# Value products of a threshold attention taken once per visit, with the last 64 keys of two heads in four 64x64 tiles, and one rotation of four PSUM banks

## The chip, the cores and the metric

One core of one Trainium2 chip. The metric is device time in microseconds (us) of one execution on that core; lower is better. TensorE's granted clock, the share of full speed that the chip's throttle allowed, was 0.982 to 0.995 over a whole run.

## The reference, cut to what matters

```python
# q, k, v: (8 batches, 8 heads, 576, 64) float32; tau = 0.02
scores = scale * np.matmul(q, k.transpose(0, 1, 3, 2))
thresh = np.max(scores, axis=-1, keepdims=True) - tau
scores = np.where(scores >= thresh, scores, -1000000000.0)
scores = scores - np.max(scores, axis=-1, keepdims=True)
attn = np.exp(scores)
attn = attn / (np.sum(attn, axis=-1, keepdims=True) + 1e-09)
attn_out = np.matmul(attn, v)
# bridge: (B, H, S, D) -> (B*S, H*D) = (4608, 512)
h = x @ w_in            # 512 x 2048
r = np.maximum(h, 0.0)
out = (r * r) @ w_out   # 2048 x 512
```

576 queries or keys are four blocks of 128 and a rest of 64. That rest is what the change is about.

## The kernel before

The kernel walks through *visits*. A visit is a pair of heads of one batch, in five *steps*: four of 128 queries for each head, and one with the last 64 queries of both. A step computes scores on TensorE, maxima and thresholds on VectorE, exponents on ScalarE and the division on GpSimd. The weights must then be transposed so that keys lie on partitions. The first visits do it on TensorE. The last 25 visits do it in two moves: VectorE transposes 32x32 squares into a buffer `turned`, and SyncE issues transfers that put the squares into their places in `wT`.

```python
NC9 = 2 * NBLK + 1                                   # 4 + 4 whole chunks, one shared chunk of last keys
wT = const.tile([P, NC9, S], FP32, name="wT")
NB = 2 * KB * 2 * 32                                 # KB = 18 blocks of 32 keys
turned = const.tile([P, 2 * NB], FP32, name="turned")   # two slots
...
def turn_blocks(vis, i):                             # VectorE, one step after the scores
    if not two or i % 2 == 0:
        at = len(blocks) % 2 * NB                    # the slots are used in turn
    ...
    for u in range(2 if two else 1):
        nc.vector.transpose(wb[:, u * KB:(u + 1) * KB, i % 2, :], w[:, u, :].rearrange("p (k q) -> p k q", q=32))

def place_blocks(vis, pair):                         # 16 transfers of SyncE
    for qb in range(4):
        for j in range(4):
            ...
            nc.sync.dma_start(out=to[:, :, at:at + 64], in_=wb[rows, j::4, :, :].rearrange("p c u q -> p c (u q)"))
```

A visit fills three such buffers: *pair 0* (steps 0 and 1), *pair 1* (steps 2 and 3) and the *rest* (step 4). With two slots, pair 0 of the next visit comes to lie where pair 1 of this visit was. VectorE may therefore turn it only when pair 1's transfers have read it.

The value products, before, came in two groups per visit, for different columns of `wT`. The fifth key chunk was padded with zeros in `vs` to 128 rows:

```python
def mix(n, cols):
    ps = bank[4] if by_dma(n) else take("tx", (4, 5))
    for c in range(NBLK + 1):
        for u in range(2):
            cw = NBLK if c == NBLK else u * (NBLK + 1) + c
            nc.tensor.matmul(ps[u * D:(u + 1) * D, 0:nq], vs[n % 2][:, u * (NBLK + 1) + c, :], wT[:, cw, cols],
                             start=(c == 0), stop=(c == NBLK))
...
mixed = {1: (0, 4), NBLK: (2, 4)}      # columns 0-255 four steps after step 1; 256-575 four after step 4
...
turn_blocks(m, x)
if x % 2 or x == NBLK:
    place_blocks(m, x // 2)
```

Between these, TensorE works off *pieces* of the feed-forward layer (one piece is 8 passes, 1.73 us; a pass is one of the two instructions of which every fp32 matmul consists), at a rate that the program works out from how many are waiting.

Of the kernel before, what the change touches and what calls it, by code (L numbers as in the profile page):

```python
# [19 lines left out]
def kernel(  # L20
# [10 lines left out]
    nc = tc.nc  # L31
# [38 lines left out]

    NC9 = 2 * NBLK + 1
# [4 lines left out]
    for i in range(2):  # L76
        nc.gpsimd.memset(vs[i], 0.0)
# [18 lines left out]
    p1s = const.tile([P, HD], FP32, name="p1s")  # L96
    u_sum = const.tile([P, HD], FP32, name="u_sum")
# [68 lines left out]
    def load_v(n):  # L166
# [4 lines left out]
        for u in range(2):  # L171
            at = u * (NBLK + 1)
            queue.dma_start(out=t[:, at:at + NBLK, :],
                              in_=v[b, h + u, 0:NBLK * P, :].rearrange("(c p) d -> p c d", p=P))
            queue.dma_start(out=t[u * D:(u + 1) * D, at + NBLK, :], in_=v[b, h + u, NBLK * P:S, :])
# [68 lines left out]
    used = {"tx": 0, "mm": 0}  # L244

    def take(what, among):
        used[what] += 1
        return bank[among[used[what] % len(among)]]

# [24 lines left out]
    blocks = {}  # L274

    def turn_blocks(vis, i):
# [12 lines left out]
        for u in range(2 if two else 1):  # L289
            nc.vector.transpose(wb[:, u * KB:(u + 1) * KB, i % 2, :], w[:, u, :].rearrange("p (k q) -> p k q", q=32))  # L290

    def place_blocks(vis, pair):

        wb = blocks[vis, pair]
        for qb in range(4):
            rows = slice(qb * 32, qb * 32 + 32)
            for j in range(4):
                to = wT[j * 32:j * 32 + 32, :, :]
                if pair < NBLK // 2:
                    at = pair * 2 * P + qb * 64  # L300
                    nc.sync.dma_start(out=to[:, :, at:at + 64], in_=wb[rows, j::4, :, :].rearrange("p c u q -> p c (u q)"))  # L301
                else:
# [4 lines left out]
                    at = NBLK * P + qb % 2 * 32  # L307
# [3 lines left out]

    def mix(n, cols):

        b, pr = divmod(visits[n][0], HP)
        nq = cols.stop - cols.start
        ps = bank[4] if by_dma(n) else take("tx", (4, 5))
        for c in range(NBLK + 1):
            for u in range(2):
                cw = NBLK if c == NBLK else u * (NBLK + 1) + c
                nc.tensor.matmul(ps[u * D:(u + 1) * D, 0:nq], vs[n % 2][:, u * (NBLK + 1) + c, :], wT[:, cw, cols],  # L320
                                 start=(c == 0), stop=(c == NBLK))
        lo = b * S + cols.start
        assert lo + nq - RING <= read_to["x"]

        def to(first, count):
            at = (lo + first) % RING
            assert at + count <= RING
            return xT[:, pr, at:at + count]

        whole = (lo % RING) + nq <= RING  # L330
        if by_dma(n):
            src = ps[:, 0:2 * P].rearrange("p (b u q) -> p b u q", u=2, b=4)
            if whole:
                nc.scalar.copy(to(0, 2 * P).rearrange("p (u b q) -> p b u q", u=2, b=4), src)  # L334
            else:

                for u in range(2):
                    fit = min(max((RING - lo % RING - u * P) // 32, 0), 4)
                    for b0, b1 in ((0, fit), (fit, 4)):
                        if b0 < b1:  # L340
                            nc.scalar.copy(to(u * P + b0 * 32, (b1 - b0) * 32).rearrange("p (b q) -> p b q", q=32),
                                           src[:, b0:b1, u, :])
            if nq > 2 * P:
                nc.scalar.copy(to(2 * P, nq - 2 * P), ps[:, 2 * P:nq])
        else:
            fit = nq if whole else RING - lo % RING
            for x0, x1 in ((0, fit), (fit, nq)):
                if x0 < x1:
                    nc.scalar.copy(to(x0, x1 - x0), ps[:, x0:x1])
# [3 lines left out]
    ring3 = [6, 5, 7]  # L353
# [7 lines left out]
    def mlp_in(j, x):  # L361

        f, at = FORDER[x], j * TCH % RING
        pair = x // 2
        if x % 2 == 0:
            used["h"] = take("mm", (6, 7)) if j < PLAIN else bank[ring3[pair % 3]]
# [55 lines left out]
    def product(j, x, half):  # L422

        if x == 0 and half == 0:
# [275 lines left out]
```

## Time and profile before

| | before |
|---|---|
| median of three runs | 1431.0 us (1430.79 to 1433.61) |
| profiled execution | 1429.3 us |
| TensorE busy | 97% |
| VectorE / ScalarE / GpSimd busy | 60% / 30% / 50% |

### The profile page before, as it was taken

To read this page: it belongs to the slowest core of one execution; us is meant where nothing else is said; L and a number is where in the kernel's file an instruction comes from. 1 tells how busy PE (TensorE), PEld (TensorE's weight loads), DVE (VectorE), ACT (ScalarE), POOL (GpSimd) and SP (SyncE) were. 2 spreads that over 40 slices of the span, in tenths; PEclk is the share of its full clock that TensorE was granted. 3 is DMA by queue.
4 is the path that set the end of the run, shared out by engine and by line. 5 is a ranking of instruction groups with operands and counts; after the bars stand their busy time and mean duration, and the time that the engine had idled before them with its cause. 6 is when DMAs were issued, how large, how long until landed. Compare 5 with 4: busy or idle time off the path is not lost.

```text
span 1429.3 us, 22123 instructions
## 1 busy us (share of the span) xinstructions
PE 1380.3 (97%) x7460; PEld 1067.1 (75%) x7460; DVE 860.0 (60%) x1781; ACT 435.2 (30%) x1063; POOL 720.3 (50%) x933
## 2 busy tenths in 40 slices
PE   5898989999999999999999999999999999999998
PEld 3676656777777777777777777778777777788887
DVE  5998986875657565657566656566656665621011
ACT  3765655223222222232223222222222232210100
POOL 3687877645464545354545445555445354531321
PEclk9998989999999999999999999999999999999999
DMA  7663441445454554454555554544455445430000
GB/s 148 128 139 102 126 120 42 76 72 101 89 100 84 106 96 95 81 106 80 103 90 110 96 95 84 109 84 96 86 110 93 92 84 107 78 71 15 0 15 15
DMA packets 503839, 125.93 MB, mean 88 GB/s; under 512 B 494928, under 2 KB 495728, under 8 KB 503728
## 3 DMA queue, kind: packets, MB, share of 16 engines
q1 hardware_dynamic: 494448, 107.42, 41.0%
q0 software_dynamic: 6896, 16.82, 3.8%
q8 instruction: 60, 0.98, 0.3%
q10 hardware_dynamic: 2384, 0.30, 0.1%
q14 instruction: 51, 0.42, 0.1%
HBM read 48.63 MB, written 9.44 MB: 41 GB/s over the span
## 4 chain that ended last, share of the span: by engine, by line
PE 81%; DVE 6%; SPq 5%; issue 3%; ACT 2%; DMA 1%; POOL 1%; ACTq 0%; DVEq 0%; POOLq 0%
PE bank L369 33%; PE bank L438 24%; PE s L201 12%; PE bank L320 10%; SPq L301 3%; SPq L308 1%; PE bank L259 1%; PE bank L403 1%; DVE w L229 1%; DVE turned L138 1%; SPq L162 1%; DVE st L206 1%; ACT wT L260 1%; DVE turned L290 1%; DVE turned L137 1%
## 5 line engine op out<-in xcount | busy, mean ns | idle before, releaser
L369 PE MATMUL bank<-xT,w_in_sb 128*128 128x256 f32 x2304 | 521.2, 383 | 1.6 <-ACT osb L410 1.6
L369 PEld LDWEIGHTS bank<-xT,w_in_sb 128*128 128x128 f32 x2304 | 432.9, 190 | 82.2 <-issue 22.3
L206 DVE TENSOR_REDUCE st<-s 128x1 f32<-128x576 f32 x288 | 207.0, 753 | 308.7 <-PE s L201 308.7
L229 DVE SCALAR_TENSOR_TENSOR w<-s,st,w 128x576 f32<-128x576 f32 x269 | 207.5, 804 | 75.6 <-ACT w L217 75.3
L241 POOL TENSOR_SCALAR w<-w,st 128x576 f32<-128x576 f32 x269 | 238.5, 894 | 26.9 <-DVE st L232 18.9
L438 PE MATMUL bank<-wo,gsum 128*128 128x256 f32 x1088 | 249.3, 382 | 0.0
L438 PEld LDWEIGHTS bank<-wo,gsum 128*128 128x128 f32 x1088 | 204.4, 190 | 38.4 <-issue 9.6
L380 POOL TENSOR_TENSOR g<-g 128x512 f32<-128x512 f32 x144 | 150.5, 1046 | 155.9 <-ACT g L379 138.5
L201 PE MATMUL s<-kT,qT 64*128 64x288 f32 x1024 | 180.2, 446 | 38.8 <-DVE w L229 16.9
L438 PE MATMUL bank<-wo,g 128*128 128x256 f32 x816 | 188.3, 381 | 0.0
L239 POOL TENSOR_SCALAR st<-st 128x2 f32<-128x2 f32 (+1 forms) x160 | 39.0, 244 | 295.5 <-DVE w L229 284.2
L217 ACT ACTIVATE w<-s,st 128x576 f32<-128x576 f32 x269 | 184.9, 733 | 0.6 <-ACT st L215 0.4
L320 PE MATMUL bank<-wT,vs 128*64 128x128 f32 (+3 forms) x1700 | 178.1, 357 | 2.6 <-ACT wT L260 2.4
L201 PEld LDWEIGHTS s<-kT,qT 64*128 64x128 f32 x1024 | 102.0, 193 | 99.7 <-issue 70.7
L438 PEld LDWEIGHTS bank<-wo,g 128*128 128x128 f32 x816 | 153.5, 190 | 27.8 <-issue 5.3
L290 DVE STREAM_TRANSPOSE turned<-w 128x576 f32<-128x576 f32 x225 | 162.1, 753 | 5.2 <-POOL w L241 5.1
L320 PEld LDWEIGHTS bank<-wT,vs 128*64 128x64 f32 x1700 | 104.7, 140 | 75.9 <-issue 22.1
L379 ACT ACTIVATE g<-bank 128x512 f32<-128x512 f32 x144 | 86.1, 598 | 205.8 <-PE bank L369 205.7
L214 ACT ACTIVATE st<-st 128x2 f32<-128x2 f32 (+1 forms) x160 | 33.3, 208 | 324.8 <-DVE st L206 324.2
L334 ACT COPY xT<-bank 128x256 f32<-128x256 f32 x42 | 15.6, 372 | 284.1 <-PE bank L320 284.1
L451 DVE TENSOR_TENSOR gsum<-g 128x512 f32<-128x512 f32 x34 | 22.6, 693 | 107.7 <-PE bank L438 107.7
L184 POOL COPY qmid<-qT 64x64 f32<-64x64 f32 x64 | 18.2, 285 | 101.8 <-DVE qT L180 99.9
(69 smaller groups left out, 963.9 us busy)
## 6 DMA issues: line engine op xcount, KB each, us to landing
wT<-turned SPq DMA_DIRECT2D x800, 72.0 KB, 2.2
ql<-in_q_dram SPq DMA_DIRECT2D x126, 72.0 KB, 2.5
out_dram<-osb POOLq DMA_DIRECT2D x34, 256.0 KB, 2.8
wo<-in_moe_w_in_dram SPq DMA_DIRECT2D x16, 512.0 KB, 4.8
wo<-in_moe_w_out_dram SPq DMA_DIRECT2D x16, 512.0 KB, 3.7
vs<-in_v_dram POOLq DMA_DIRECT2D x50, 128.0 KB, 3.5
kl<-in_k_dram SPq DMA_DIRECT2D x63, 72.0 KB, 2.4
kl<-in_k_dram SPq DMA_DIRECT2D x63, 64.0 KB, 2.3
```

What stands on the lines that cost most here:

```text
L201: nc.tensor.matmul(sc[u][:, half, 0:HALF], lhsT, kT[rows, half * HALF:(half + 1) * HALF], start=True, stop=True)
L206: nc.vector.tensor_reduce(out=mx[:, u:u + 1], in_=sc[u][:, :, 0:HALF], axis=AX.XY, op=ALU.max)
L217: nc.scalar.activation(out=w[:, u, :].rearrange("p (h k) -> p h k", h=2), in_=sc[u][:, :, 0:HALF], func=AF.Exp, bias=bias[:, u:u + 1], sca ...
L229: nc.vector.scalar_tensor_tensor(out=wu, in0=sc[u][:, :, 0:HALF], scalar=thr[:, u:u + 1], in1=wu, op0=ALU.is_ge, op1=ALU.mult, accum_out=s ...
L241: nc.gpsimd.tensor_scalar(out=w[:, u, :], in0=w[:, u, :], scalar1=z[:, u:u + 1], scalar2=rcp[:, u:u + 1], op0=ALU.add, op1=ALU.mult)
L290: nc.vector.transpose(wb[:, u * KB:(u + 1) * KB, i % 2, :], w[:, u, :].rearrange("p (k q) -> p k q", q=32))
L301: nc.sync.dma_start(out=to[:, :, at:at + 64], in_=wb[rows, j::4, :, :].rearrange("p c u q -> p c (u q)"))
L320: nc.tensor.matmul(ps[u * D:(u + 1) * D, 0:nq], vs[n % 2][:, u * (NBLK + 1) + c, :], wT[:, cw, cols], start=(c == 0), stop=(c == NBLK))
L369: nc.tensor.matmul(h[:, x % 2, :], w_in_sb[:, c, f * P:(f + 1) * P], xT[:, c, at:at + TCH], start=(c == 0), stop=(c == NMC - 1))
L379: nc.scalar.activation(out=to, in_=h, func=AF.Relu)
L380: nc.gpsimd.tensor_tensor(out=to, in0=to, in1=to, op=ALU.mult)
L438: nc.tensor.matmul(to, left[:, f, :], wo[:, slot, f, :], start=(f == 0), stop=(f == HF - 1))
```

## The change

The intent is to save TensorE time, which sets the end. The last 64 keys of the two heads, for two column groups (320 and 256 columns), become four matmuls on the four 64x64 quarters of the array at once, in place of four padded ones on two halves. For that, all products of a visit are taken together, after its last block. V's last rows are loaded into both halves of the partitions (two transfers in place of one), and VectorE's transposes are split so that the last keys land in the right halves. The feed-forward banks, the products and the value products share one rotation of four banks; one copy (`p5s`) and two additions on GpSimd make that possible.

```diff
-    for i in range(2):
-        nc.gpsimd.memset(vs[i], 0.0)
...
+    p5s = const.tile([P, HD], FP32, name="p5s")
...
-            queue.dma_start(out=t[u * D:(u + 1) * D, at + NBLK, :], in_=v[b, h + u, NBLK * P:S, :])
+            for half in range(2):
+                queue.dma_start(out=t[half * D:(half + 1) * D, at + NBLK, :], in_=v[b, h + u, NBLK * P:S, :])
...
+    def next_bank():
+        among = (4, 5, 6, 7) if state["step"] > first_dma + 2 else (6, 7)
+        used["bank"] = min([x for x in among if x > used["bank"]] or among)
+        return bank[used["bank"]]
...
+        if two and i >= 2:
+            parts = [(0, 0, KB - 2, 0), (0, KB - 2, KB, KB), (1, 0, 2, KB - 2), (1, 2, KB, KB + 2)]
+        else:
+            parts = [(u, 0, KB, u * KB) for u in range(2 if two else 1)]
...
+        one, two = (next_bank() for x in range(2))
+        for c in range(NBLK):
+            for ps, at in ((one[:, 0:N1], 0), (two[:, 0:S - N1], N1)):
+                for u in range(2):
+                    term(ps, u, c, at, first=(c == 0))
+
+        for ps, at, places in ((one[:, 0:N1], 0, (above, below)), (two[:, 0:S - N1], N1, (below, above))):
+            for u, rows in enumerate(places):
+                term(ps, u, NBLK, at, rows, last=True)
... (products: three fixed banks -> next_bank(); "5" copied to p5s, two additions to nc.gpsimd)
-            mixed = {1: (0, 4), NBLK: (2, 4)}
+            mixed = {NBLK: (0, 4)}
...
-            if x % 2 or x == NBLK:
-                place_blocks(m, x // 2)
+            if x >= 2:
+                place_blocks(m, x - 2)
```

More of the change, by code (lines that the diff above doesn't have):

```diff
@@ L242, in divide @@
                                     scalar2=rcp[:, u:u + 1], op0=ALU.add, op1=ALU.mult)
-    used = {"tx": 0, "mm": 0}
+    used = {"tx": 0, "mm": 0, "bank": 7}
     def take(what, among):
@@ L274 @@
     blocks = {}
+    N1 = 2 * P + REST
     def turn_blocks(vis, i):
@@ L288, in turn_blocks @@
         wb = blocks[vis, i // 2]
-        for u in range(2 if two else 1):
-            nc.vector.transpose(wb[:, u * KB:(u + 1) * KB, i % 2, :], w[:, u, :].rearrange("p (k q) -> p k q", q=32))
+        if two and i >= 2:
+            parts = [(0, 0, KB - 2, 0), (0, KB - 2, KB, KB), (1, 0, 2, KB - 2), (1, 2, KB, KB + 2)]
+        else:
+            parts = [(u, 0, KB, u * KB) for u in range(2 if two else 1)]
+        for u, k0, k1, at in parts:
+            nc.vector.transpose(wb[:, at:at + k1 - k0, i % 2, :],
+                                w[:, u, k0 * 32:k1 * 32].rearrange("p (k q) -> p k q", q=32))
     def place_blocks(vis, pair):
@@ L299, in place_blocks @@
                 if pair < NBLK // 2:
-                    at = pair * 2 * P + qb * 64
+                    at = pair * N1 + qb * 64
                     nc.sync.dma_start(out=to[:, :, at:at + 64], in_=wb[rows, j::4, :, :].rearrange("p c u q -> p c (u q)"))
@@ L306, in place_blocks @@
                     n = len(range(first, KB, 4))
-                    at = NBLK * P + qb % 2 * 32
+                    at = 2 * P + qb % 2 * 32
                     nc.sync.dma_start(out=to[:, c:c + n, at:at + 32], in_=wb[rows, first::4, 0, :])
     read_to = {"x": 0}
-    def mix(n, cols):
-        b, pr = divmod(visits[n][0], HP)
-        nq = cols.stop - cols.start
-        ps = bank[4] if by_dma(n) else take("tx", (4, 5))
-        for c in range(NBLK + 1):
-            for u in range(2):
-                cw = NBLK if c == NBLK else u * (NBLK + 1) + c
-                nc.tensor.matmul(ps[u * D:(u + 1) * D, 0:nq], vs[n % 2][:, u * (NBLK + 1) + c, :], wT[:, cw, cols],
-                                 start=(c == 0), stop=(c == NBLK))
-        lo = b * S + cols.start
-        assert lo + nq - RING <= read_to["x"]
-        def to(first, count):
-            at = (lo + first) % RING
-            assert at + count <= RING
-            return xT[:, pr, at:at + count]
-        whole = (lo % RING) + nq <= RING
-        if by_dma(n):
-            src = ps[:, 0:2 * P].rearrange("p (b u q) -> p b u q", u=2, b=4)
-            if whole:
-                nc.scalar.copy(to(0, 2 * P).rearrange("p (u b q) -> p b u q", u=2, b=4), src)
-            else:
-                for u in range(2):
-                    fit = min(max((RING - lo % RING - u * P) // 32, 0), 4)
-                    for b0, b1 in ((0, fit), (fit, 4)):
-                        if b0 < b1:
-                            nc.scalar.copy(to(u * P + b0 * 32, (b1 - b0) * 32).rearrange("p (b q) -> p b q", q=32),
-                                           src[:, b0:b1, u, :])
-            if nq > 2 * P:
-                nc.scalar.copy(to(2 * P, nq - 2 * P), ps[:, 2 * P:nq])
-        else:
-            fit = nq if whole else RING - lo % RING
-            for x0, x1 in ((0, fit), (fit, nq)):
-                if x0 < x1:
-                    nc.scalar.copy(to(x0, x1 - x0), ps[:, x0:x1])
@@ L353, with put, to @@
-    ring3 = [6, 5, 7]
+    def put(n, first, ps, by_32s):
+        b, pr = divmod(visits[n][0], HP)
+        count = ps.shape[1]
+        lo = (b * S + first) % RING
+        assert b * S + first + count - RING <= read_to["x"]
+        def to(x0, x1):
+            at = (lo + x0) % RING
+            return xT[:, pr, at:at + x1 - x0]
+        fit = min(RING - lo, count)
+        if not by_32s:
+            for x0, x1 in ((0, fit), (fit, count)):
+                if x0 < x1:
+                    nc.scalar.copy(to(x0, x1), ps[:, x0:x1])
+            return
+        src = ps.rearrange("p (b u q) -> p b u q", u=2, b=4)
+        if fit == count:
+            nc.scalar.copy(to(0, count).rearrange("p (u b q) -> p b u q", u=2, b=4), src)
+            return
+        for u in range(2):
+            b0 = min(max((fit - u * P) // 32, 0), 4)
+            for x0, x1 in ((0, b0), (b0, 4)):
+                if x0 < x1:
+                    nc.scalar.copy(to(u * P + x0 * 32, u * P + x1 * 32).rearrange("p (b q) -> p b q", q=32),
+                                   src[:, x0:x1, u, :])
@@ new lines, in mix, with term @@
+    def mix(n, cols):
+        def term(ps, u, c, at, rows=slice(0, P), first=False, last=False):
+            nc.tensor.matmul(ps[u * D:(u + 1) * D, :], vs[n % 2][rows, u * (NBLK + 1) + c, :],
+                             wT[rows, NBLK if c == NBLK else u * (NBLK + 1) + c, at:at + ps.shape[1]],
+                             start=first, stop=last)
+        above, below = slice(0, D), slice(D, P)
+        if not by_dma(n):
+            ps = take("tx", (4, 5))[:, 0:cols.stop - cols.start]
+            for c in range(NBLK):
+                for u in range(2):
+                    term(ps, u, c, cols.start, first=(c == 0))
+            for u, rows in enumerate((above, below)):
+                term(ps, u, NBLK, cols.start, rows, last=True)
+            put(n, cols.start, ps, False)
+            return
+        one, two = (next_bank() for x in range(2))
+        for c in range(NBLK):
+            for ps, at in ((one[:, 0:N1], 0), (two[:, 0:S - N1], N1)):
+                for u in range(2):
+                    term(ps, u, c, at, first=(c == 0))
+        for ps, at, places in ((one[:, 0:N1], 0, (above, below)), (two[:, 0:S - N1], N1, (below, above))):
+            for u, rows in enumerate(places):
+                term(ps, u, NBLK, at, rows, last=True)
+        put(n, 0, one[:, 0:2 * P], True)
+        put(n, NBLK * P, one[:, 2 * P:N1], False)
+        put(n, 2 * P, two[:, 0:S - N1], True)
@@ L363, in mlp_in @@
         f, at = FORDER[x], j * TCH % RING
-        pair = x // 2
         if x % 2 == 0:
-            used["h"] = take("mm", (6, 7)) if j < PLAIN else bank[ring3[pair % 3]]
+            used["h"] = take("mm", (6, 7)) if j < PLAIN else next_bank()
         h = used["h"].rearrange("p (f n) -> p f n", f=2)
@@ L422, in product @@
     def product(j, x, half):
-        if x == 0 and half == 0:
-            a, c, b = ring3[2], ring3[0], ring3[1]
-            used["abc"] = a, b, c
-            ring3[:] = [b, a, c]
-        a, b, c = (bank[y][:, 0:HD] for y in used["abc"])
+        if half == 0:
+            used["p"] = next_bank()
+        to = used["p"][:, 0:HD]
         p = PRODUCTS[x]
@@ L433, in product @@
         g0, g1 = g[:, 0:HF, :], g[:, HF:, :]
-        left, slot, to = {
-            "1": (g0[:, :, 0:P], Q00, a), "5": (gsum[0], FT1, c), "6": (gsum[1], FT2, b), "2": (g1[:, :, 0:P], Q10, a),
-            "7": (gsum[0], FT3, b), "4": (g1[:, :, P:], FT4, a), "3": (gsum[1], Q11, c)}[p]
+        left, slot = {"1": (g0[:, :, 0:P], Q00), "5": (gsum[0], FT1), "6": (gsum[1], FT2), "2": (g1[:, :, 0:P], Q10),
+                      "7": (gsum[0], FT3), "4": (g1[:, :, P:], FT4), "3": (gsum[1], Q11)}[p]
         for f in range(half * HF // 2, (half + 1) * HF // 2):
@@ L448, in then @@
             if p == "1":
-                nc.scalar.copy(p1s, a)
+                nc.scalar.copy(p1s, to)
             elif p == "5":
+                nc.scalar.copy(p5s, to)
                 halves(lambda f: tt(out=gsum[0][:, f, :], in0=g0[:, f, 0:P], in1=g0[:, f, P:], op=sub))
             elif p == "6":
-                tt(out=u, in0=b, in1=p1s, op=add)
-                tt(out=osb[:, 0, HD:], in0=c, in1=u, op=add)
+                tt(out=u, in0=to, in1=p1s, op=add)
+                nc.gpsimd.tensor_tensor(out=osb[:, 0, HD:], in0=p5s, in1=u, op=add)
                 halves(lambda f: tt(out=gsum[1][:, f, :], in0=g1[:, f, 0:P], in1=gsum[1][:, f, :], op=sub))
             elif p == "2":
-                tt(out=osb[:, 0, 0:HD], in0=a, in1=p1s, op=add)
+                tt(out=osb[:, 0, 0:HD], in0=to, in1=p1s, op=add)
             elif p == "7":
-                tt(out=u, in0=b, in1=u, op=add)
-                tt(out=osb[:, 1, HD:], in0=c, in1=u, op=add)
+                tt(out=u, in0=to, in1=u, op=add)
+                nc.gpsimd.tensor_tensor(out=osb[:, 1, HD:], in0=p5s, in1=u, op=add)
             elif p == "4":
-                tt(out=osb[:, 1, 0:HD], in0=u, in1=a, op=sub)
+                tt(out=osb[:, 1, 0:HD], in0=u, in1=to, op=sub)
                 return [lambda: store_rows(j, 1, 2)]
             else:
-                tt(out=osb[:, 0, HD:], in0=c, in1=osb[:, 0, HD:], op=add)
+                tt(out=osb[:, 0, HD:], in0=to, in1=osb[:, 0, HD:], op=add)
                 return [lambda: store_rows(j, 0, 1)]
```

## The prediction

> **What bounds the kernel now.** I read the page from the top, then one stage table, then the timeline of TensorE over one visit, then the queue of SyncE. The page's engine shares and slices come first.
>
> ```profile
> span 1429.3 us, 22123 instructions
> PE 1380.3 (97%) x7460; PEld 1067.1 (75%) x7460; DVE 860.0 (60%) x1781; ACT 435.2 (30%) x1063; POOL 720.3 (50%) x933
> PE   5898989999999999999999999999999999999998
> PEclk9998989999999999999999999999999999999999
> ```
>
> TensorE is busy throughout, at full clock after the first slices, and every other engine has a third or more free. Busy need not mean useful, so next the steady stage as one window (its length, then busy time of PE, its weight loads, DVE, ACT, POOL, then clock and DMA):
>
> ```profile
> 288.00:1260.00 972.00, 969.62 (x5011) 750.29 (x5010) 609.03 (x1289) 261.36 (x653) 475.71 (x656) 1.00 0.51 93
> ```
>
> and whom TensorE waited for in the whole run (total us, times, longest):
>
> ```profile
> PE s L201 <- DVE w L229: 17.7, 12, 3.7
> PE s L201 <- DVE kT L180: 14.1, 4, 8.5
> PE s L201 <- DVE wo L229: 7.7, 5, 3.0
> PE bank L320 <- ACT wT L260: 2.4, 10, 0.2
> ```
>
> In 972 us TensorE lacks 2.4 us. The waits are nearly all in the first 280 us, where weights are still being rounded. So in the steady stage time is the sum of TensorE's passes, and no wait is there to be saved: a change pays what it takes from that sum. One visit (a head pair, five steps) on TensorE:
>
> ```profile
> 812.94 1.24 PE L201 MATMUL s<-kT,qT 64*128 64x288 f32 x8
> 814.11 2.38 PE L320 MATMUL bank<-wT,vs 128*64 128x256 f32 x20
> 816.42 3.72 PE L438 MATMUL bank<-wo,gsum 128*128 128x256 f32 x16
> ...
> 836.62 1.24 PE L201 MATMUL s<-kT,qT 64*128 64x288 f32 x8
> 837.79 2.91 PE L320 MATMUL bank<-wT,vs 128*64 128x320 f32 x20
> 840.64 1.56 PE L369 MATMUL bank<-xT,w_in_sb 128*128 128x256 f32 x6
> ```
>
> Each fp32 matmul is two instructions (passes). Start to start, the value products of 256 columns take 816.42-814.11 = 2.31 us for 20 passes, those of 320 columns 840.64-837.79 = 2.85 us: 5.16 us a visit. Narrow windows of this timeline show passes starting two at a time, every 0.216 us (256 columns) and 0.269 us (320): the two heads share the array as two 128x64 tiles. Ten slots make 2.16 and 2.69; the other 0.15 us of each group are tile changes (about 0.10 to leave, 0.05 for the first weights).
>
> Then the queue that brings the weights of those products, SyncE:
>
> ```profile
> 800.03 19.70 SPq L301 DMA_DIRECT2D wT<-turned  x24
> 819.84 10.55 SPq L308 DMA_DIRECT2D wT<-turned  x16
> 830.43 1.76 SPq L162 DMA_DIRECT2D kl<-in_k_dram  x3
> ...
> 836.00 24.32 SPq L301 DMA_DIRECT2D wT<-turned  x32
> 860.41 10.26 SPq L308 DMA_DIRECT2D wT<-turned  x16
> ```
>
> It issues without a break: a visit's 48 transfers at 0.61+0.04 us each and 10 loads fill some 38.4 of the 40.95 us between the same points of two visits. It is the second bound, hidden today because the transfers of one half visit go while the other half is still used.
>
> **What the Trainium skill says.** "TensorEngine Tiling (Array Packing)", Key Properties: tiles work independently, and changing the tiling mode drains the engine; 64x64 gives four tiles. The trace agrees on the drain: from a 128x64 to a 64x64 group at 122.4 us the start comes 0.097 us later than the passes need, and the next slot 0.045 late. "TensorE: Matmul & The Clock Gate", Part 3, What overlaps and what doesn't: matmuls start and end strictly in program order. If so, four products of two passes each could not run as four tiles, for the second pass of the first stands ahead of the second product. The trace disagrees:
>
> ```profile
> 78.36 0.96 PE L201 MATMUL s<-kT,qT 64*128 64x288 f32 x5
> 78.96 0.40 PE L265 MATMUL bank<-ident,wo 64*128 64x64 f32 x4
> 79.17 0.40 PE L201 MATMUL s<-kT,qT 64*128 64x288 f32 x1
> ```
>
> Four transposes on one row tile start before a score pass that stands ahead of them in the program on the other tile. So it runs ahead by tile, at least four matmuls deep; four tiles need about six. "DMA: Bandwidth & Descriptors", Anatomy of one DMA: about 2 us fixed per transfer, mostly completion; here 1.9 to 2.2 us from issue to landing for these transfers.
>
> **The change part by part.**
> 1. Last keys in four tiles. Before, the fifth key chunk holds 64 real keys of each head padded with zeros to 128 rows: two slots each of 256 and 320 columns. After, the two heads and the two column groups are four 64x64 tiles: two slots of 320. Slots before: 10 x 0.2157 + 10 x 0.2692 = 4.85 us; after: 8 x 0.2157 + 8 x 0.2692 + 2 x 0.2692 = 4.42. Saved 0.43 us.
> 2. One visit at once. One entry and exit of the 128x64 mode goes (0.15); one change to 64x64 inside comes (0.097+0.045 = 0.14). Net 0.01. Together 0.44 us x 25 visits = 11.0 us less on TensorE, all on the path.
> 3. The transposed visits at the start (35 small groups) also get the 64x64 ending with no columns saved: 0.14 x 28 (the 7 last ones are already followed by 64x64 work) = 4 us of TensorE, in a stage with 36 us of TensorE gaps; I count +2.
> 4. Bank rotation, and two VectorE additions per chunk moved to GpSimd (34 in all), with 34 more copies and adds on ScalarE and GpSimd: a bank is used again only after three others have been filled, 3 x 3.45 us (16 passes of 0.216); drains are 0.4 to 0.7 us. No wait before, none after: 0. The 100 more small VectorE transposes at about 0.1 us (estimate) sit in a 60% busy engine: 0.
> 5. Timing of the transfers. Before, pair 0's transfers go two steps after its queries, pair 1's and the last block's in the two following steps, and each half's products use other columns of wT. After, all 48 transfers of a visit must start after the products of the visit before have ended, and land before its own start. Loop: about 0.3 us to start, 47 x 0.653 = 30.7 to the last issue, 1.3 for the roughly one-us delays that hit this queue once in 24 us, 1.9 landing, 0.1 to start: 34.3 us (estimate). On the other side stands the work of TensorE between the products: counted from the kernel's own filling rule, 17 pieces of feed-forward (8 passes, 1.73 us) plus scores (4 x 1.37 + 1.06, with tile changes) = 35.9 us in most visits, but 16 pieces = 34.1 in nine, and 30.4 in the last visit, where no scores are left and one more chunk is left to the end. The waits: 9 x 0.2 + 3.9 = 5.7 us.
>
> Sum: -11.0 + 2 + 5.7, and about -1 for the three small waits at 525, 608 and 1033 us, which the same queue made: -4.3 us, so 1426.7; I say 1426.
>
> **The rivals.**
> A. The four tiles do not run together, but two by two (ordering, or two row tiles into the same partitions). For: the skill's sentence on order; no 64x64 group of four exists in this trace. Against: the run-ahead above, and score passes that already write two banks from two row tiles. It would return the 0.54 us of the last keys: 25 x 0.54 = 13.5, and the time would be about 1440.
> B. The transfer loop becomes the bound. For: the slack is 1.6 us in a good visit and negative in nine; a loop of 36.5 in place of 34.3 would cost 9 x 2.4 + 14 x 0.65 + 6 = 37 us, time about 1457. The buffer of turned blocks is a second way in: VectorE must wait for pair 1's landing (some 23 us after the products) before it turns the next visit's first block, due at 21 to 24 us, with 1.1 to 4 us until the next scores need its threshold. At 525 us this chain (queue, landing, transposes, kT) already cost 1.8 us. Against: a wait there also gives the queue time, so the waits overlap and do not add.
> C. The loop fits better than I think and the whole 11 us plus the small waits come: 1417 to 1419.
> D. Chunks become ready only once per group of four visits, so TensorE could run dry. Counted from the filling rule: it never does, 90 in place of 60 pieces are left after the last products, and that work is only moved to the end.
>
> **Range and chances.** The best case is limited by the 11 us and the few waits, about 1416. The bad side is longer: rival A alone 1440, and half of rival B 1438. Range 1416 to 1440. Two per cent faster would be 1402.4, for which no part has the size: 0.02. Two per cent slower, 1459.6, needs the loop two us longer than estimated, or A and B together: 0.04. Within: 0.94.
>
> **What would show it.** Step 1: in the timeline, a group of 8 passes 64*64 of 256 and 320 columns that takes about 0.55 to 0.6 us from its start to the next mode's end (1.1 under A), and value products of 4.7 us in one group per visit. Step 3: 0.14 us more per small group before 290 us. Step 4: no waits of TensorE for ScalarE or VectorE at the banks. Step 5: TensorE's waits for the transfers of wT, or for VectorE behind them, at the value products or scores: under 10 us in all, the largest at the last visit near the end. I am wrong if these waits exceed 15 us, if four tiles show a 1.1 us ending, or if the pieces between products differ from 16 and 17.

## More of the kernel before

A window's columns are its length, then busy time (with the number of instructions) of PE, its weight loads, DVE, ACT and POOL, then the granted clock, the share of DMA and its rate in GB/s:

```profile
290.00:1200.00 910.00, 907.62 (x4693) 702.36 (x4692) 570.95 (x1210) 244.03 (x610) 444.31 (x617) 1.00 0.51 94
```

What VectorE waited for in this window (who, for whom: total us, times, longest us):

```profile
DVE st L206 <- PE s L201: 260.4, 109, 4.9
...
DVE turned L290 <- POOL w L241: 2.9, 3, 2.0
```

VectorE never waits there for a transfer. SyncE's queue, from 300 to 1240 us, waits mostly for VectorE:

```profile
SPq L301 <- DVE turned L290: 62.1, 23, 5.2
```

That is slack: once a visit the queue has nothing to send, for 2.7 us on average. And GpSimd's issues of the last 64 rows of V (line, engine, what, count, then busy us and mean ns):

```profile
L175 POOL DMA_DIRECT2D vs<-in_v_dram x50 | 26.9, 539 | 0.0
```

## The result, and the profile after

| | before | after |
|---|---|---|
| median of four runs | 1430.89 us (1429.49 to 1433.61) | 1438.84 us (1437.98 to 1441.71) |
| profiled execution | 1429.3 us | 1436.5 us |
| ratio | 1 | 1.0057 (95%: 1.0036 to 1.0077) |

Ratios here are the mean time of one kernel's fast runs over the mean of the other's in the same rounds, so not quite the ratio of the medians. The change lost 0.6%, some 7 to 8 us. That lies inside the predicted range and inside "within 2%", but 4.3 us less had been predicted and the sign is wrong. The page after:

```profile
span 1436.5 us, 22320 instructions
PE 1381.1 (96%) x7460; PEld 1066.3 (74%) x7460; DVE 855.2 (60%) x1847; ACT 440.0 (31%) x1080; POOL 772.3 (54%) x1015
```

TensorE is busy as long as before (1380.3 us), though its work should have shrunk by 11 us, and GpSimd works 52 us more. TensorE over the products of one visit (start, length, what, number of passes):

```profile
820.73 4.79 PE L359 MATMUL bank<-wT,vs 128*64 128x320 f32 x40
825.45 2.86 PE L468 MATMUL bank<-wo,gsum 128*128 128x256 f32 x12
```

Start to start, the 40 passes take 825.45-820.73 = 4.72 us, in place of 5.16 in two groups. The trace's records of the eight passes of the last keys start at 824.763, .770, .776 and .783, then at 825.043, .050, .083 and .090, and the next mode at 825.449. All four tiles run at once. So the array's part of the prediction came to the hundredth. It does not show in the end, because TensorE is no longer full in the steady stage (the window of 290 to 1200 us):

```profile
290.00:1200.00 910.00, 901.32 (x4686) 695.79 (x4687) 572.22 (x1282) 249.20 (x628) 487.64 (x687) 1.00 0.52 96
```

It lacks 8.7 us of 910 here, where before it lacked 2.4. Part of the loss also counts as busy: the score groups of 8 passes take 1.17 us from start to start when the two heads run side by side, but 1.5 to 1.9 us when the second head's bank comes free later than the first's. In this window that was so for 14 of 111 groups, before for one. So score groups took 133.95 us in place of 126.17. Who made TensorE late? VectorE's waits in this window:

```profile
DVE st L207 <- PE s L202: 203.0, 104, 4.0
...
DVE turned L303 <- DMA wT<-turned: 25.1, 16, 2.6
DVE turned L303 <- POOL w L242: 6.2, 7, 2.1
```

The line of the DMA is new: 16 times, 25.1 us in all, VectorE stands before a transpose into `turned` until a transfer that reads the slot has landed. The timelines of SyncE, VectorE and TensorE show one of these:

```profile
422.37 21.72 SPq L316 DMA_DIRECT2D wT<-turned  x32
...
444.19 10.70 SPq L323 DMA_DIRECT2D wT<-turned  x16
```

```profile
447.04 1.44 DVE L303 STREAM_TRANSPOSE turned<-w 128x576 f32<-128x576 f32 x2 [2.27 <-DMA wT<-turned]
448.40 1.25 DVE L482 TENSOR_TENSOR gsum<-g 128x512 f32<-128x512 f32 x2
449.57 0.81 DVE L230 SCALAR_TENSOR_TENSOR w<-s,st,w 128x576 f32<-128x576 f32 x1
...
450.31 0.81 DVE L230 SCALAR_TENSOR_TENSOR w<-s,st,w 128x576 f32<-128x576 f32 x1
```

```profile
450.54 1.94 PE L202 MATMUL s<-kT,qT 64*128 64x288 f32 x8 [1.84 <-DVE w L230]
```

The square brackets hold the idle time before a group and what ended it. Read it as a loop. The products end at about 422 and set the queue free. It needs 21.72 us to issue pairs 0 and 1, and by the trace's records the last transfer of pair 1 lands 2.6 us later, at 446.67. Only then may VectorE turn pair 0 of the next visit, at 447.04. Behind that, in its own order, stand two subtractions for the feed-forward layer and the two thresholds. These free the score banks, so the next scores start at 450.54, 1.84 us late. One step later come the next products (458.96), though their own transfers had all landed by 456.14, and the round begins again: 458.96-417.04 = 41.9 us from products to products, while TensorE's work in it (16 pieces, scores, 4.72 us of products) is 38.8 us.

That the queue's partner changed is seen in its own waits, 300 to 1240 us:

```profile
SPq L316 <- PE bank L359: 54.9, 24, 6.9
```

In place of VectorE's transposes it now waits for the end of the products. The last visit shows the other loop, the one that the prediction had looked at. The last line is a window in the form used above, with the granted clock third from the end:

```profile
1264.57 0.75 PE L359 MATMUL bank<-wT,vs 128*64 128x320 f32 x2
1268.42 6.44 PE L359 MATMUL bank<-wT,vs 128*64 128x320 f32 x38 [3.10 <-DMA wT<-turned]
1274.79 1.56 PE L402 MATMUL bank<-xT,w_in_sb 128*128 128x256 f32 x6
```

```profile
1268.40:1274.80 6.40, 6.38 (x39) 3.72 (x39) 0.00 (x0) 0.00 (x0) 0.00 (x0) 0.73 0.01 3
```

The products took 10.22 us in place of 4.72, 5.5 us more. Not all of it is waiting: the last transfer landed at 1268.22, 3.65 us after the products had begun. After that, the trace grants TensorE only 0.50 of its clock for 3.41 us, from 1269.7, which at half speed costs some 1.7 us (an estimate from these two numbers). And GpSimd issues twice as many loads of V's last rows, by whose side TensorE waits once for a sum that GpSimd makes late (at 366.14 us):

```profile
L176 POOL DMA_DIRECT2D vs<-in_v_dram x100 | 53.3, 545 | 0.0
```

```profile
PE bank L468 <- POOL gsum L392: 1.8, 2, 1.5
```

A balance of the two profiled executions. I compared the start of each visit's last product group, with 1.727 us taken off for every piece done more by then, so that only array time and waits are left:

| part | us | predicted |
|---|---|---|
| start, up to the first such group (at 296 us in the change) | -2.7 | +2 |
| array: 0.43 to 0.44 for each of 25 visits | -10.85 | -11.0 |
| waits in the steady stage, net of those before | +14.3 | +1.8 - 1 |
| last visit: the wait (3.65) and the half clock after it | +5.5 | +3.9 |
| last store | +1.0 | 0 |
| sum | +7.2 | -4.3 |

Of the 14.3 us, 8.5 fall to the first five visits, which hold 16 pieces each; visits of 17 pieces mostly run at 40.52 us a visit without a wait.

### The profile page after: what moved, and what is told of

Its sections match the earlier page's. It is cut to its first block, busy times and chain, and to the rows that moved or that the text cites. A ratio compares the mean times of both kernels' runs of the same rounds, so it can differ in the third digit from the quotient of the medians.

```text
span 1436.5 us, 22320 instructions
## 1 busy us (share of the span) xinstructions
PE 1381.1 (96%) x7460; PEld 1066.3 (74%) x7460; DVE 855.2 (60%) x1847; ACT 440.0 (31%) x1080; POOL 772.3 (54%) x1015
## 4 chain that ended last, share of the span: by engine, by line
PE 59%; SPq 6%; issue 1%; DMA 1%; DVE 1%; POOL 1%; POOLq 0%; DVEq 0%
PE bank L402 24%; PE bank L468 21%; PE s L202 7%; PE bank L359 7%; SPq L316 5%; DMA wT<-turned 1%; SPq L323 1%; DVE turned L303 0%; DVE w L230 0%; POOL vs L176 0%; POOL g L413 0%; DVE gsum L486 0%; POOL vs L173 0%; DVE kT L181 0%; POOL gsum L392 0%
## 5 line engine op out<-in xcount | busy, mean ns | idle before, releaser
L202 PE MATMUL s<-kT,qT 64*128 64x288 f32 x1024 | 185.7, 443 | 39.0 <-DVE w L230 19.1
L303 DVE STREAM_TRANSPOSE turned<-w 128x576 f32<-128x576 f32 (+2 forms) x325 | 168.8, 565 | 44.2 <-DMA wT<-turned 31.2
L202 PEld LDWEIGHTS s<-kT,qT 64*128 64x128 f32 x1024 | 105.3, 192 | 102.8 <-issue 75.0
L359 PE MATMUL bank<-wT,vs 128*64 128x128 f32 (+7 forms) x1700 | 172.5, 361 | 5.9 <-DMA wT<-turned 3.1
L215 ACT ACTIVATE st<-st 128x2 f32<-128x2 f32 (+1 forms) x160 | 33.4, 209 | 418.8 <-DVE st L207 418.3
L359 PEld LDWEIGHTS bank<-wT,vs 128*64 128x64 f32 (+1 forms) x1700 | 99.7, 138 | 80.2 <-issue 32.3
```

What stands on the lines that cost most here:

```text
L202: nc.tensor.matmul(sc[u][:, half, 0:HALF], lhsT, kT[rows, half * HALF:(half + 1) * HALF], start=True, stop=True)
L303: nc.vector.transpose(wb[:, at:at + k1 - k0, i % 2, :], w[:, u, k0 * 32:k1 * 32].rearrange("p (k q) -> p k q", q=32))
L359: nc.tensor.matmul(ps[u * D:(u + 1) * D, :], vs[n % 2][rows, u * (NBLK + 1) + c, :], wT[rows, NBLK if c == NBLK else u * (NBLK + 1) + c, a ...
```

## The experiments

All kernels ran five rounds against the kernel before on the same chip. A ratio is always against the runs of the kernel before in the same session, so runs of different sessions are compared by their ratios.

The main theory, T, is the loop just read: the two-slot buffer ties VectorE to the landing of pair 1. Against it stood R1, that the rotation of banks, with the work moved to GpSimd, costs time itself; R2, that the last keys' tiles, with their loads and small transposes, cost as much as they save, or more; and R3, that SyncE's queue just has too much to send, in whatever arrangement. H came after the first four runs: the tiles save what was predicted, but their helpers take part of it back.

**A third slot.** Pair 0, pair 1 and the rest get a slot each. Pair 0 of the next visit then waits only for pair 0's own 16 transfers, which stand first in the queue, and not for pair 1's behind them.

```diff
-    turned = const.tile([P, 2 * NB], FP32, name="turned")
+    turned = const.tile([P, 2 * NB + KB * 32], FP32, name="turned")
-            at = len(blocks) % 2 * NB
+            at = i // 2 * NB
```

> The changed kernel with a third, small buffer for turned blocks, so that VectorE never turns a block of the next visit into a buffer whose transfers may still be under way. Theory T (the loss is the loop products - transfers - landing - VectorE's turning - threshold - next scores): the 25 us that VectorE waits for landings in the steady stage goes to about 0, TensorE's steady waits fall from some 14 us to about 3, the wait at the last visit (5.5 us) stays; 1428 us, ratio to before 0.998. Rival R1 (the loss comes from the bank rotation and the additions moved to GpSimd): no change, 1438.

Measured: 1425.6 us (1422.63 to 1428.42), ratio 0.9973 (0.9951 to 0.9994). Against the 1.0057 of the change that is 0.84%, or 12 us. VectorE's waits in the window of 290 to 1200 us, all of those at the transposes:

```profile
DVE turned L303 <- POOL w L242: 6.2, 6, 2.1
```

The waits for landing are gone, 25.1 us to none, and of 114 score groups in the window only two take over 1.3 us. Waits of the steady stage in the balance fell from 14.3 to 4.8 us. T holds for some 9.5 us of its 14.3. What is left are small waits, the last visit's, and the change is now a small gain.

**Zero padding again.** The change without the four tiles: one group per visit, padded chunks, half the loads, no split transposes.

```diff
+        nc.gpsimd.memset(vs[i], 0.0)        # for both vs
-            for half in range(2):
-                queue.dma_start(out=t[half * D:(half + 1) * D, at + NBLK, :], in_=v[b, h + u, NBLK * P:S, :])
+            queue.dma_start(out=t[u * D:(u + 1) * D, at + NBLK, :], in_=v[b, h + u, NBLK * P:S, :])
-        if two and i >= 2:
+        if False:
-                term(ps, u, NBLK, at, rows, last=True)    # four 64-row terms
+                term(ps, u, NBLK, at, last=True)          # four 128-row terms
```

> The changed kernel with the last keys of the value products padded with zeros to 128 rows again (two 128x64 tiles in place of four of 64x64); all else as changed. T: the group of value products grows from 4.72 to 5.00 us, and since it lies on TensorE's path and inside the transfer loop alike, all of 25 x 0.28 = 7 us shows: 1446 us. Rival R2 (four tiles save nothing that counts): 1439.

Measured: 1435.81 us (1433.13 to 1437.64), ratio 1.0043 (1.0023 to 1.0063). A miss: it should have lost the 7 us that the tiles save on the array, and is not slower than the change at all. On the array it is as expected:

```profile
819.06 5.07 PE L360 MATMUL bank<-wT,vs 128*64 128x320 f32 x40
824.06 3.29 PE L469 MATMUL bank<-wo,gsum 128*128 128x256 f32 x14
```

5.00 us a visit in place of 4.72, so 25 x 0.28 = 7.0 us more. Something that came with the tiles seems to cost about as much. VectorE's waits for landing are here 18.5 us in place of 25.1, and TensorE's wait for GpSimd's sum near 366 us is 0.3 in place of 1.5 us. That gave H, which three kernels below test.

The two traces show another reason, against the expectation that the 0.28 us lies inside the loop as well. With padding, SyncE's first transfer of a round starts 4.71 us after the start of the products (median of 24 visits), 0.30 before their end. With four tiles it starts 4.81 us after their start, 0.09 after their end. Pair 0 overwrites columns that only the group of 320 reads. Padded, this group ends before that of 256; in four tiles both end together. So the tiles shorten TensorE's work and not the loop, and where the loop is the bound they save nothing, by this reading. TensorE's waits in the steady stage, in the balance, are 6.7 us here and 14.3 in the change.

**Only the rotation.** The kernel before with `next_bank`, `p5s` and the additions on GpSimd, products in two groups as before.

```diff
-        ps = bank[4] if by_dma(n) else take("tx", (4, 5))
+        ps = next_bank() if by_dma(n) else take("tx", (4, 5))
... (and the rotation's other lines, as in the change)
```

> The kernel before with only the bank rotation, the extra copy on ScalarE and the two additions per chunk on GpSimd. T: 1430 us (same as before within 2 us), no landing waits of VectorE. R1: slower than before by a good part of 8 us, 1435 or more.

Measured: 1430.41 us (1428.0 to 1431.34), ratio 1.0004 (0.9984 to 1.0025). No cost or gain is seen, and the interval allows a cost of at most 3.6 us: R1 is out as the cause of the 8 us, and step 4 of the prediction holds for this part.

**A third slot, and a quarter of the transfers on ScalarE's queue.** Meant to shorten the queue's round.

```diff
     (the third slot, and:)
-                place_blocks(m, x - 2)
+                place_blocks(m, x - 2, (0, 1, 2), nc.sync)
+        if 0 < s <= NST and by_dma(steps[s - 1][0]) and steps[s - 1][1] >= 2:
+            place_blocks(steps[s - 1][0], steps[s - 1][1] - 2, (3,), nc.scalar)    # after the exponents
```

> Third buffer, and a quarter of the transfers (4 of each 16) issued from ScalarE's queue after its exponents, so SyncE issues 36 in place of 48 per visit, 7.9 us less in the loop. T: neither the loop by VectorE nor the one by the queue binds; steady waits near 0 and the last visit's wait gone: 1439 - 14 - 5 = 1420 us, ratio 0.992. R1: no better than 1436. If ScalarE's issues (2.6 us at a time) delay exponents or drains, some of it comes back as waits of scores for thresholds.

Measured: 1486.6 us (1479.68 to 1489.54), ratio 1.0393 (1.0368 to 1.0417). A clear miss. SyncE's queue, 300 to 1240 us:

```profile
SPq L316 <- DMA wT<-turned: 254.4, 94, 7.5
```

SyncE now waits 254 us for *transfers*, where it had none of this. The trace's records of the transfers name the semaphore that each waits for and raises. Both queues take theirs from the same eight, in the order of the program, and each transfer waits until the one eight before it has landed. ScalarE's transfer that raises one of these was issued at 872.29, late, since ScalarE itself was held up for 6.38 us before; SyncE's next transfer, which takes the same semaphore, followed at 874.53, a landing time later, after a pause of over 6 us. So two queues that were meant to run side by side go in lockstep, with the later one setting the pace. The run is no evidence on whether a shorter queue would help.

**A third slot, and zero padding.** The edits of the first two experiments together.

> Third buffer and last keys padded with zeros (no four tiles, no extra loads of V, transposes not split). T with four tiles worth 25 x 0.28 us: 7 us slower than the third buffer with four tiles, 1433 us, ratio to before 1.002. Theory H (what four tiles save on TensorE is eaten by what they need: two more loads of V per visit on GpSimd's queue and transposes in four pieces): 1426, ratio 0.997.

Measured: 1430.73 us (1426.52 to 1432.68), ratio 1.0003 (0.9984 to 1.0022). With the third slot the tiles are worth 1.0003 - 0.9973 = 0.3%, or 4.3 us (from two sessions). It lies between the 7 us of the array and none. The two intervals overlap, and the difference is about as large as its own uncertainty (0.3%), so neither end is clearly excluded.

**Zero padding, and the loads of V kept at 100.** Two loads per visit more on GpSimd than padding needs. They put values where zeros should be, so this kernel's result is wrong (relative error 0.38); its time is what counts.

```diff
     (zero padding, but with:)
             for half in range(2):
                 queue.dma_start(out=t[half * D:(half + 1) * D, at + NBLK, :], in_=v[b, h + u, NBLK * P:S, :])
```

> The padded version with the two extra loads of V per visit put back on GpSimd's queue; the padding is then overwritten, so the result is wrong on purpose. T: as the padded version, 1436. H by GpSimd's queue (1.1 us a visit ahead of its next division): 3 to 5 us more, 1440.

Measured: 1439.84 us (1438.65 to 1441.56), ratio 1.0070 (1.0052 to 1.0088). Against 1.0043 without the loads: 0.27%, 3.9 us, from two sessions whose intervals overlap. TensorE's wait for GpSimd's sum at this place is back as well, 1.4 us in place of 0.3. So it is likely that the loads take part of the tiles' gain, as H has it, but that is not shown. In the balance, TensorE's waits of the steady stage are 8.3 us here and 6.7 without the loads.

Nor is it shown how they would do it. In the change's trace, the transfers of pairs 0 and 1 that had no load of V under way beside them (452 of them in 290 to 1200 us) landed 2.30 us after issue on average, and the 109 with six such loads under way took 3.71 us. So the loads may also lengthen loop T. No run separates this from their time on GpSimd.

**Zero padding, and the transposes split in four.** The pieces go where the whole ones would.

```diff
     (zero padding, but with the split kept:)
+            parts = [(0, 0, KB - 2, 0), (0, KB - 2, KB, KB - 2), (1, 0, 2, KB), (1, 2, KB, KB + 2)]
```

> The padded version with the transposes of the third and fourth block in four pieces again, each to the place it had. T: as the padded version, 1436. H by VectorE: 3 to 5 us more, 1440.

Measured: 1436.45 us (1433.31 to 1440.62), ratio 1.0044 (1.0022 to 1.0067), as without the split. The small transposes cost nothing that can be seen.

**The change with two useless transfers per visit.** They stand behind pair 0's transfers in SyncE's queue, read a part of q and write a scratch tile, and so lengthen the loop of T by about 1.3 us a visit.

```diff
+    scratch = const.tile([32, 2, 9, 32], FP32, name="scratch")
                 place_blocks(m, x - 2)
+                if x == 2:
+                    for z in range(2):
+                        nc.sync.dma_start(out=scratch[:, z, :, :], in_=q[0, z, 0:S // 2, 0:32].rearrange("(c p) d -> p c d", p=32))
```

> The changed kernel with two useless transfers (0.65 us each to issue) in SyncE's queue behind pair 0 of every visit, inside the transfer loop. T: the loop is 1.3 us longer, and it binds in 16-piece visits and is within a us of binding in the others: 15 to 25 us more, about 1458. R1 (the loss has nothing to do with the queue): no change.

Measured: 1458.89 us (1452.87 to 1460.45), ratio 1.0197 (1.0174 to 1.022); 20 us more than the change. VectorE's wait for landing, 290 to 1200 us:

```profile
DVE turned L304 <- DMA wT<-turned: 55.9, 22, 3.5
```

25.1 us in 16 waits became 55.9 in 22. Of the 25 x 1.3 = 33 us put into the queue, 20 reach the end. A loop with slack would have swallowed them. The transfers lengthen the loop through the products just as much; but in this window TensorE never stands before its products for a transfer, so the growth is T's.

**The kernel before with the same two transfers.**

```diff
                 place_blocks(m, x // 2)
+                if x == 1:
+                    for z in range(2):
+                        nc.sync.dma_start(...)      # the same transfers
```

> Control: the kernel before with the same two useless transfers behind pair 0 of every visit. T: its queue is full for 38.4 of 40.95 us a visit, and no loop closes through the products, so 1.3 us more fit: 1430 to 1434 us. Rival R3 (any more work in that queue costs 25 to 30 us, in either kernel): 1450 to 1460.

Measured: 1430.31 us (1429.08 to 1434.4), ratio 1.0011 (0.9994 to 1.0027). The queue's slack took them up:

```profile
SPq L302 <- DVE turned L291: 38.8, 21, 4.8
```

62.1 us of waiting for VectorE became 38.8. The same 33 us cost 20 us in one arrangement and at most 4 us (by the interval) in the other. R3 is out: not the amount to send, but the place of the products in the round makes the queue the bound.

**A third slot, and three pieces held back for the last visit.** The filling rule keeps three pieces of work, so that TensorE has something to do while the last transfers land.

```diff
     (the third slot, and:)
-                best = min(best, have / (e - s))
+                best = min(best, (have - (3 * PIECE_US if e == END and s < END - 5 else 0)) / (e - s))
```

> Third buffer, and three pieces of feed-forward held back for the five steps before the last products (20 in place of 17 pieces there, 16 in place of 17 in a few visits before). T: the wait of some 5 us in the last products goes, 0.2 to 0.5 us each come back in three or four visits: 3 to 5 us less than the third buffer alone, ratio to before 0.994 to 0.995. Rival: the wait there is not the queue's lateness, no change, 0.997.

Measured: 1424.4 us (1417.93 to 1428.3), ratio 0.996 (0.9937 to 0.9982). The last visit's wait is gone from the trace:

```profile
1257.59 4.79 PE L359 MATMUL bank<-wT,vs 128*64 128x320 f32 x40
1262.30 8.04 PE L402 MATMUL bank<-xT,w_in_sb 128*128 128x256 f32 x36
```

No stretch at half clock follows there either. In time it is 0.13% better than the third slot alone, which the intervals do not tell from nothing.

**A third slot, and the loads of V later.** They go behind the division of the third step, when GpSimd has less waiting, in place of the visit's end.

```diff
     (the third slot, and:)
-            elif last and more and n >= 2 * HP:
+            elif last and more and 2 * HP <= n < 3 * HP - 2:
                 load_v(n + 1)
+            elif at == 2 and by_dma(n):
+                load_v(n)
```

> Third buffer, and V of a visit loaded two steps of its own later (end of its third step) in place of the end of the visit before, so that GpSimd's issues no longer stand ahead of the division and sums of the first step. H by GpSimd's queue: the 4 us that the padded version lost with two more loads come back, at least the stall of 1.7 us for gsum: 2 to 4 us less than the third buffer alone, 0.995. T alone: no change, 0.997.

Measured: 1424.52 us (1420.37 to 1427.47), ratio 0.9967 (0.9947 to 0.9986). TensorE's wait for GpSimd's sum between 330 and 400 us, 1.5 us with the third slot alone, is now:

```profile
PE bank L468 <- POOL gsum L392: 0.2, 1, 0.2
```

The time can't be told from that of the third slot alone. The wait moved in the trace, and its worth in time stays open.

**All three.** Third slot, pieces held back, loads later.

> Third buffer, held pieces and late loads of V together. T with H: the gains add up, 6 to 8 us less than the third buffer alone, 1418 us, ratio to before 0.992.

Measured: 1420.86 us (1418.13 to 1424.59), ratio 0.9942 (0.9925 to 0.996). It beats the kernel before by 0.58% (8.3 us) and the change by 1.15%. Over the third slot alone that is 0.31%, by ratios of two sessions whose intervals still overlap a little, so the two small parts together are likely worth something, but that is not shown.

| kernel | ratio to before | 95% |
|---|---|---|
| the change | 1.0057 | 1.0036 to 1.0077 |
| rotation only | 1.0004 | 0.9984 to 1.0025 |
| padded | 1.0043 | 1.0023 to 1.0063 |
| padded, loads kept | 1.0070 | 1.0052 to 1.0088 |
| padded, split kept | 1.0044 | 1.0022 to 1.0067 |
| the change, two transfers more | 1.0197 | 1.0174 to 1.022 |
| before, two transfers more | 1.0011 | 0.9994 to 1.0027 |
| third slot | 0.9973 | 0.9951 to 0.9994 |
| third slot, padded | 1.0003 | 0.9984 to 1.0022 |
| third slot, ScalarE's queue | 1.0393 | 1.0368 to 1.0417 |
| third slot, pieces held | 0.9960 | 0.9937 to 0.9982 |
| third slot, loads later | 0.9967 | 0.9947 to 0.9986 |
| all three | 0.9942 | 0.9925 to 0.9960 |

## Why the prediction was right or wrong

- **Steps 1 and 2, the array: right.** 4.72 us a visit against 4.71 from the sum, and four passes within 20 ns. Rival A, two by two, is out. The inference that TensorE runs ahead by tile, taken from four small transposes in the trace before, carried over to four tiles of two passes each.
- **Step 3, the transposed visits: not settled.** +2 was predicted; the balance shows -2.7. But up to there the trace grants TensorE only half its clock for 27.3 us in the profile before and for 20.5 us in the one after. Half of the difference, 3.4 us (an estimate, for a TensorE that is busy throughout), is more than this term. The kernel with the third slot, with 13.7 us at half clock, comes to its first steady product group at 291.63 us, and the change at 296.46.
- **Step 4, the side effects: half right.** No cost of the rotation, the additions and the small transposes was seen (1.0004, and 1.0044 against 1.0043). The extra loads of V were not in the sum at all, and may cost 3.9 us, which is not clear of noise. They sit on GpSimd, which is 54% busy, and the prediction priced only the instructions that it moved there. Six loads of a visit, issued in a row from 357.95 to 361.69 us, come before work that TensorE needs.
- **Step 5, the timing of the transfers: wrong, and it turned the sign.** Both loops were named, and only one was counted. That one, through the products, was sized right. From the end of the products to the landing of the last of the next 48 transfers the change's trace has 33.4 to 35.1 us, 34.1 on average (34.3 predicted), against 34.1, 35.8 or, in the last visit, 30.5 us of work (34.1, 35.9 and 30.4 predicted). In 21 of 23 steady visits all had landed before TensorE came to the products, and never was one over 0.3 us late. In the last visit the transfers came 3.65 us late (3.9 predicted); the half clock after it was not foreseen. The step that failed is the other loop, VectorE's wait for pair 1's landing. It stood under rival B with its numbers (some 23 us after the products, due at 21 to 24) and was then set aside with the sentence that a wait there also gives the queue time, "so the waits overlap and do not add". So 1.8 us of waits were put for the steady stage, where the trace has 14.3, of which some 9.5 went with the third slot. The runs show the reverse of the sentence. The queue cannot use the time, since its next round starts only when the products have ended, and these are behind the late scores: in the visit shown, the transfers had landed 2.8 us before the products began. The wait for landing closes a loop of its own, 41.9 us long there, where TensorE's work is 38.8. Taking it away gave back 12 us; lengthening it by 1.3 us a visit cost 20.
- **Its sign of being wrong,** over 15 us of waits for transfers or for VectorE behind them, was met only if all of the balance's 14.3 and 3.65 us counts; 4.8 of them stayed when that loop was cut.
- **A reading of the lines:** SyncE's queue did not issue "without a break" before. The 32 transfers at 836.00 us took 24.32 us, where 32 x 0.653 is 20.9, and the waits for VectorE make 2.7 us a visit. This slack is what the control with two more transfers used.
- **Rival C: not reached,** but 8.3 of its 11 us came once the buffer, the last visit and the loads were looked after. **Rival D, running dry: not seen;** no wait of TensorE in the steady stage is for want of a chunk.
- **The range** held since its bad side had been drawn for half of rival B, 1438: that was near what came. Its end, 1440, came from rival A, which did not occur, so it held in part by luck.

Open: why the balance still has 4.8 us of waits in the steady stage with the third slot, and whether any of it belongs to the loads of V. No run takes all of it away.

## What to carry to other kernels

When a change makes work start later in a round (here all transfers after the products in place of half of them), draw the round for every buffer that the moved work reads and writes, not only for the one that it feeds; each is a loop of its own, and the longest counts. Then compare each loop's length with the work of the bounding engine between the same two points: with one or two us of slack in 40, a saving outside the loop is worth at most the slack. And look at which instruction starts the next round: here the four tiles ended the products sooner, but did not let the transfers start sooner. That an engine is half idle does not prove that more work on it is free. Ask what stands behind the added instructions in its order.

## What the Trainium skill lacked or had wrong

- "TensorE: Matmul & The Clock Gate", Part 3, What overlaps and what doesn't, says that matmuls start and end strictly in program order. In the program the two last-key products of 320 columns come before the two of 256, with two passes each. But the first passes of all four start at 824.763 to 824.783, the second passes of the two later products at 825.043 and 825.050, and those of the two earlier ones at 825.083 and 825.090. So a later product's second pass started before an earlier one's: starts are in order within a tile, not across tiles.
- The same page, Back-to-back issue gap, has N/2.4 + 2.5 ns for a matmul alone and no line for fp32, whose passes the skill counts elsewhere without a time. In these runs each of the two passes of an fp32 matmul takes 0.2157 us at 256 columns and 0.2692 at 320, which is N/1.2 + 2.5 ns a pass.
- "TensorEngine Tiling (Array Packing)", Key Properties, says that a change of mode drains the array, without a figure. Here it was 0.09 to 0.10 us, and 0.05 to 0.10 more at the next slot.
- "DMA: Bandwidth & Descriptors", Issuing engines are not separate DMA queues, says that issuing from several engines only saves the sequencer's time, which is usually small beside the transfer. Here it was not small: one transfer takes 0.65 us of SyncE and lands in 2.2, so 32 of them take 21.72 us to issue, which is most of the way from the products to pair 1's landing (23.8 us on average).
- No page tells that queues of two engines can hold each other up through completion semaphores which they share. With a quarter of the transfers on ScalarE's queue, SyncE waited 254.4 us for landings, and the kernel took 56 us longer than before. It is a property of how this program's semaphores are handed out, and the trace's records show it.
